# Retention and soft MoE on one core: half of the queries stay unscaled, y of three more pairs is turned by VectorE, two more key blocks are turned on chip

## The chip, the cores and the metric

The kernel runs on one core of a Trainium2 chip. The metric is the device time of one execution in microseconds; the kernel before has 152.23 us as the median of three runs (152.21 to 153.1). Below, PE is TensorE, DVE is VectorE, ACT is ScalarE, POOL is GpSimd and SP is SyncE, whose queue issues every DMA of this kernel.

## The reference

A retention layer (a linear recurrence with one decay per head) is followed by a soft mixture of experts, all in float32. Batch is 4, heads 8, sequence 768, head size 64; 32 slots, 8 experts, hidden width 1024.

```
for t in range(S):                     # per batch b and head h
    state = gamma * state + outer(k[t], v[t])
    y[t] = q[t] @ state / sqrt(64)
x = y as (4 * 768, 512)
logits = x @ phi                        # 3072 x 32
d = softmax over tokens;  slot_input = d.T @ x
slot_out[e] = relu(slot_input[e] @ w1[e]) @ w2[e]
out = softmax over slots (logits) @ slot_out
```

## The kernel before, in words

The sequence is cut into 6 chunks of 128 tokens. A step is one chunk of one batch, so there are 24 steps; two steps make a pair P, and the main loop runs over 12 pairs. Order is written by hand: every engine executes its instructions in the order of the Python code, so what stands ahead of a line on its engine is ahead of it on the chip.

In a pair, `carry_mm` multiplies the state by the queries, `attend_mm` adds the masked scores times the values, both into the PSUM banks Y0 and Y1, and `attend_copy` brings them to SBUF as `yT` (features by tokens): ACT the groups 0 and 1 (L305), DVE the groups 2 and 3 (L306). Then come `state_mm` and `state_add` (the state, bank S), and `turn_k` for the keys of the next pair. The host gives keys as features by tokens. The state needs them as tokens by features, too: for steps in `TURNED` TensorE turns them (L232) and ACT copies the result (L233), for the others the host sends them a second time and they are loaded beside the rest (`WITHK`, 512 more columns, 256 KB, in the pair's load).

The dispatch (`dispatch_u`, L424) needs y as tokens by features. There are two ways. `natural_mm` turns it on TensorE (L330, eight turns a pair) and ACT copies it (L337). `block_turn` lets DVE turn 32 by 32 blocks in place (L341), and `block_moves` puts the blocks in their places with 16 copies of 32 x 256 (L351), by ACT and POOL in turn. Pairs in `MOVED` (0, 2, 4, 6, 8) go the second way.

Decay: `decay_q` multiplies the queries of a step by the table `qtab` on POOL (L238), `decay_v` the values by powers of gamma (L243), `next_chunk` brings `qtab` to the next chunk (L246). The logits of four steps are made at odd pairs (`logits_mm`, L368), the dispatch of the four steps before them just ahead.

Loads all stand in SP's queue, in the order in which the code issues them: pair P + 3 at step P (three buffers, so it waits until pair P has been used, L227 and L221) and expert weights (`load_two`, 2 MB each, L174), as `PACE` says. After the loop, `hidden` (L667) and the second expert layer (L753) run on TensorE, the combine (L729) follows, ACT and DVE copy it out (L737), and SP stores it in eleven DMAs (L740).

Of the kernel before, what the change touches and what calls it, by code (L numbers as in the profile page):

```python
# [17 lines left out]
C = 128  # L18
# [10 lines left out]
HC = C // 2  # L29
# [14 lines left out]
NIN = 3  # L44
NRING = 9
PACE = (0, 1, 0, 1, 1, 1, 1, 1, 1, 0, 1, 0)
TURNED = (0, 1, 2, 3, 4, 6, 8, 10, 11, 12, 13, 14, 16, 18, 19)
SIW = 48
MOVED = (0, 2, 4, 6, 8)
WITHK = [[i for i in (2 * P, 2 * P + 1) if i not in TURNED and i < NSTEP - B] for P in range(NPP)]  # L50
ROWS = [[P for P in range(1, NPP - B // 2) if len(WITHK[P]) == n] for n in range(3)]
KINDS = [n for n in range(3) if ROWS[n]]
# [14 lines left out]
def constants():  # L67
    g = 1.0 - 2.0 ** (-5.0 - np.arange(H, dtype=np.float64))
    p = np.arange(128)
    k = np.zeros((128, K_PHI), np.float64)  # L70
    t = (np.arange(NC)[None, :, None] * C + p[:, None, None]).astype(np.float64)
    k[:, K_VSC:K_VSC + 48] = (g[None, None, :] ** -t).reshape(128, 48)
    gq = g[2 * np.arange(NPAIR)[None, :] + p[:, None] // HC]
    gy = g[head_of(p[:, None] // HC, np.arange(NPAIR)[None, :])]
    k[:, K_YT:K_YT + 64] = (gy[:, :, None] ** (8 * np.arange(16)) / np.sqrt(D)).reshape(128, 64)
    k[:, K_YT + 64:K_YT + 96] = (gy[:, :, None] ** np.arange(8)).reshape(128, 32)
    k[:, K_QT:K_QT + 64] = (gq[:, :, None] ** (C + 8 * np.arange(16)) / np.sqrt(D)).reshape(128, 64)
    k[:, K_QT + 64:K_QT + 96] = (gq[:, :, None] ** np.arange(8)).reshape(128, 32)
    k[:, K_GC:K_GC + NPAIR] = gq ** C
    k[:, K_J:K_J + GRP] = (p[:, None] // NSLOT) == np.arange(GRP)[None, :]  # L80
    return k.astype(np.float32)

# [2 lines left out]
def retention_soft_moe_kernel(  # L85
# [143 lines left out]
    def turn_k(i, name):  # L229
        kp = bank(name)  # L230
        for g in range(NPAIR):
            nc.tensor.transpose(kp[:, g * 128:(g + 1) * 128], st[i]["kT"][:, g, :], ident)  # L232
        nc.scalar.copy(st[i]["kn"], kp.rearrange("p (h d) -> p h d", d=D))  # L233

    def decay_q(i):
        q = st[i]["qT"]
        if i >= B:
            nc.gpsimd.tensor_tensor(q, q, qtab, ALU.mult)  # L238

    def decay_v(i, vsc=vsc, hs=((0, H),)):  # L240
        for a, b in hs:
            v = st[i]["v"][:, a:b]
            nc.gpsimd.tensor_tensor(v, v, vsc[:, i // B, a:b].unsqueeze(2).broadcast_to([128, b - a, D]), ALU.mult)  # L243

    def next_chunk():
        nc.gpsimd.tensor_tensor(qtab, qtab, gc.unsqueeze(2).broadcast_to([128, NPAIR, C]), ALU.mult)  # L246

    def score_mm(i):
        s = st[i]
# [40 lines left out]
    def attend_copy(P):  # L290
        y = pr[P]["yT"] = slot().rearrange("p (i g t) -> p i g t", i=2, t=C)
        for k in range(2):
            st[2 * P + k]["yT"] = y[:, k]
        if P < B // 2:
            for b in range(2):
                gb = slice(2 * b, 2 * b + 2)
                nc.vector.tensor_tensor(y[:, :, gb, :], pr[P]["Y"][b],
                                        ytab[:, gb, :].unsqueeze(1).broadcast_to([128, 2, 2, C]), ALU.mult)
            return
        if P == NPP - 1:  # L300
            for k in range(2):
                nc.scalar.copy(y[:, k, 0:2, :], pr[P]["y"][k][0])
                nc.vector.tensor_copy(y[:, k, 2:4, :], pr[P]["y"][k][1])
            return
        nc.scalar.copy(y[:, :, 0:2, :], pr[P]["Y"][0])  # L305
        nc.vector.tensor_copy(y[:, :, 2:4, :], pr[P]["Y"][1])  # L306

    def state_mm(P):
        S_ = pr[P]["S"] = bank("S").rearrange("p (i g e) -> p i g e", i=2, e=D)
# [7 lines left out]
    def state_add(P):  # L317
        for k in range(2):
            d = sst[(2 * P + k) % B]
            if P < B // 2:  # L320
                nc.scalar.copy(d, pr[P]["S"][:, k])
            else:
                nc.vector.tensor_tensor(d, d, pr[P]["S"][:, k], ALU.add)

    def natural_mm(P, ks=(0, 1), names=("A2", "A3")):
        X = pr[P].setdefault("X", {})
        for k in ks:
            X[k] = bank(names[k])
            for g in range(NPAIR):
                nc.tensor.transpose(X[k][:, g * 128:(g + 1) * 128], pr[P]["yT"][:, k, g, :], ident)  # L330
# [8 lines left out]
    def block_turn(P):  # L339
        x = pr[P]["xb"] = slot()  # L340
        nc.vector.transpose(x, pr[P]["yT"].rearrange("p i g t -> p (i g t)"))  # L341

    def block_moves(P, part):
        if part == 0:
            xn = pr[P]["xn"] = slot()
            for k in range(2):
                st[2 * P + k]["xn"] = xn[:, k * 512:(k + 1) * 512]
        x = pr[P]["xb"].rearrange("p (m b d) -> p m b d", b=4, d=32)
        xn = pr[P]["xn"].rearrange("p (m a d) -> p m a d", a=4, d=32)
        for n, (a, b) in enumerate((a, b) for a in (2 * part, 2 * part + 1) for b in range(4)):  # L350
            (nc.scalar.copy if n % 2 else nc.gpsimd.tensor_copy)(xn[32 * b:32 * b + 32, :, a], x[32 * a:32 * a + 32, :, b])  # L351

    gs = {}

# [146 lines left out]
    for P in range(NPP):  # L501
        last = P == NPP - 1
        g = P // 2
        if P == 0:
            load_one()
        if PACE[P] and P != NPP - 1 - NIN:
            load_two()
        if P == NPP - 2:
            take_w1(w1k[-1], load_half(slot()))
        if last:  # L510
            load_behind(P - 1)
        if P + NIN < NPP:
            load_pair(P + NIN)
            if P == NPP - 1 - NIN:
                load_two()
        else:
            weight_pool[0] = inp
        if not last:
            for i in (2 * P + 2, 2 * P + 3):
                decay_q(i)  # L520
            if P % 2 == 0 and 0 < P < NPP - 2:
                next_chunk()
            for i in (2 * P + 2, 2 * P + 3):
                decay_v(i)
            if P == 1:
                for a in range(4):
                    qd = slice(32 * a, 32 * a + 32)
                    nc.gpsimd.tensor_copy(rep[qd].rearrange("p (j s) -> p j s", s=NSLOT),
                                          ident[qd, 32 * a:32 * a + 32].unsqueeze(1).broadcast_to([32, GRP, NSLOT]))
        if P == 0:  # L530
            score_mm(2)
            attend_copy(0)
            score_mask(2)
            state_mm(0)
            state_add(0)
            score_mm(3)
            score_mask(3)
            turn_k(2, "sm")
            turn_k(3, "A0")
            decay_table(qtab, K_QT)  # L540
            block_turn(0)
            continue
        carry_mm(P)
        if last:
            take_w1(w1k[-1], load_half(sall))
        attend_mm(P)
        if last:
            load_behind(P)
            break
        attend_copy(P)  # L550
        if P < NPP - B // 2:
            state_mm(P)
            state_add(P)
        for k in range(2):
            if 2 * P + 2 + k in TURNED:
                turn_k(2 * P + 2 + k, ("A2", "Y0")[k] if P in MOVED else f"A{k}")
        if P == NPP - 2:
            block_moves(P - 2, 1)
            score_mm(2 * P + 2)
            score_mask(2 * P + 2)  # L560
            turn_mm(g - 1, "A2")
            turn_copy(g - 1)
            natural_mm(P, names=("S", "sm"))
            natural_copy(P)
            logits_bank(NGRP - 1)
            score_mm(2 * P + 3)
            score_mask(2 * P + 3)
            continue
        if P in MOVED:
            if P - 2 in MOVED:  # L570
                block_moves(P - 2, 1)
        else:
# [260 lines left out]
```

## Time and profile before

| what | value |
|---|---|
| median of the runs | 152.23 us |
| profiled execution, its own time | 152.43 us |
| its span, first to last instruction | 150.6 us |
| TensorE busy | 140.2 us, 93% of the span |
| VectorE, ScalarE, GpSimd busy | 57%, 38%, 49% |
| moved by DMA | 60.58 MB, of which 6.29 MB written |
| share of 16 DMA engines' time of the data queue | 95.8% |

Shares of busy time are averages over the whole span. Where an engine waits, the views of its waits and of the chain name what ended last. A DMA share of 1.00 means that all 16 DMA engines were moving packets throughout the stretch. A DMA counts as landed when its last part has arrived.

### The profile page before, as it was taken

How to read it: one execution, taken by the hardware profiler on the slowest of the kernel's cores; microseconds unless marked ns; L12 is line 12 of the kernel's file. 1: busy time of each engine (PE TensorE's matmuls, PEld its weight loads, DVE VectorE, ACT ScalarE, POOL GpSimd, SP SyncE). 2: the span in 40 equal slices, each digit the busy share in tenths (PEclk: the TensorE clock that was granted, in tenths of full speed). 3: DMA queues.
4: the chain of work that ended last, by engine and by line, in shares of the span. 5: the costliest groups of instructions: out<-in, count | busy, mean ns of one | idle time of the engine just before them, and what ended most of it. 6: DMA issues, size and time to landing. Idle time of an engine off the chain costs nothing.

```text
span 150.6 us, 5505 instructions
## 1 busy us (share of the span) xinstructions
PE 140.2 (93%) x2398; PEld 103.8 (69%) x2398; DVE 85.4 (57%) x192; ACT 57.0 (38%) x138; POOL 74.2 (49%) x107
## 2 busy tenths in 40 slices
PE   7999999989999999999998997999999999999830
PEld 2678989877999789978998786965232465556510
DVE  0397737792949487867869596557510101563350
ACT  3123462629172824555272708342420000352240
POOL 1182499969999989497395799700200000000000
PEclk9999999999999999999999999999999999999996
DMA  4999999999999999999999999999999999799696
GB/s 127 418 444 405 431 441 417 418 423 434 407 424 421 430 422 426 435 410 421 426 426 418 439 426 422 400 425 417 402 444 422 418 431 431 305 393 403 256 373 255
DMA packets 6936, 60.58 MB, mean 402 GB/s; under 512 B 768, under 2 KB 768, under 8 KB 3712
## 3 DMA queue, kind: packets, MB, share of 16 engines
q1 hardware_dynamic: 6912, 60.23, 95.8%
q8 instruction: 19, 0.31, 0.8%
q14 instruction: 5, 0.04, 0.1%
HBM read 53.93 MB, written 6.29 MB: 400 GB/s over the span
## 4 chain that ended last, share of the span: by engine, by line
PE 60%; DMA 26%; POOL 6%; DVE 2%; issue 2%; SPq 1%; DVEq 0%; POOLq 0%
DMA b<-in_xw_dram 12%; DMA b<-in_x_dram 10%; PE A L753 10%; PE A L253 8%; PE Y L286 8%; PE Y L667 5%; PE A L667 5%; PE S L314 4%; DMA r<-in_head_dram 3%; PE Y L277 3%; PE A L232 2%; POOL b L243 2%; PE A L330 2%; PE sm L368 2%; POOL b L238 2%
## 5 line engine op out<-in xcount | busy, mean ns | idle before, releaser
L261 DVE TENSOR_TENSOR r<-A,mi 128x512 f32<-128x512 f32 (+1 forms) x50 | 30.2, 663 | 20.3 <-PE A L253 20.3
L238 POOL TENSOR_TENSOR b<-b,qtab 128x512 f32<-128x512 f32 x20 | 25.3, 1287 | 14.0 <-DMA b<-in_x_dram 11.4
L253 PE MATMUL A<-b 64*128 64x128 f32 x384 | 25.7, 281 | 1.0 <-POOL b L238 0.8
L253 PEld LDWEIGHTS A<-b 64*128 64x128 f32 x384 | 22.8, 188 | 4.5 <-issue 1.6
L243 POOL TENSOR_TENSOR b<-b,kt 128x512 f32<-128x512 f32 x23 | 23.8, 1052 | 0.8 <-DMA b<-in_x_dram 0.8
L286 PE MATMUL Y<-r,b 128*64 128x128 f32 x352 | 22.4, 277 | 0.3 <-POOL b L243 0.3
L286 PEld LDWEIGHTS Y<-r,b 128*64 128x64 f32 x352 | 19.1, 137 | 2.7 <-issue 1.2
L351 POOL COPY r<-r 32x256 f32<-32x256 f32 x40 | 15.7, 392 | 1.6
L351 ACT COPY r<-r 32x256 f32<-32x256 f32 x40 | 16.1, 403 | 0.6
L753 PE MATMUL A<-b,r 128*32 128x128 f32 (+1 forms) x352 | 14.8, 304 | 0.1
L753 PEld LDWEIGHTS A<-b,r 128*32 128x32 f32 x352 | 9.7, 109 | 6.5 <-issue 4.2
L737 ACT COPY b<-A 128x384 f32<-128x384 f32 x10 | 4.5, 483 | 17.5 <-PE A L729 15.8
L277 PE MATMUL Y<-b,sst 64*64 64x128 f32 x304 | 10.6, 276 | 0.0
L314 PE MATMUL S<-b 128*64 128x64 f32 x304 | 10.5, 222 | 0.0
L314 PEld LDWEIGHTS S<-b 128*64 128x64 f32 x304 | 10.2, 138 | 0.0
L277 PEld LDWEIGHTS Y<-b,sst 64*64 64x64 f32 x304 | 8.2, 132 | 1.2
L470 POOL TENSOR_TENSOR cn<-cn,cz 128x128 f32<-128x128 f32 x6 | 2.4, 399 | 11.6 <-DVE cz L469 11.0
L462 ACT ACTIVATE cn<-cn 128x128 f32<-128x128 f32 x6 | 1.9, 310 | 16.4 <-DVE cn L461 16.4
L233 ACT COPY b<-A 128x512 f32<-128x512 f32 x10 | 5.8, 588 | 5.4 <-PE A L232 2.7
L306 DVE COPY r<-Y 128x512 f32<-128x512 f32 x9 | 6.2, 686 | 1.8 <-PE Y L286 1.7
L368 PEld LDWEIGHTS sm<-r,kt 128*32 128x32 f32 x192 | 5.3, 110 | 2.7 <-issue 2.7
L330 PE MATMUL A<-mi,r 128*128 128x128 f32 x48 | 6.6, 277 | 0.5 <-ACT r L305 0.4
(160 smaller groups left out, 207.9 us busy)
## 6 DMA issues: line engine op xcount, KB each, us to landing
b<-in_wtwo_dram SPq DMA_DIRECT2D x12, 2048.0 KB, 16.8
b<-in_x_dram SPq DMA_DIRECT2D x5, 1792.0 KB, 13.5
b<-in_x_dram SPq DMA_DIRECT2D x3, 1536.0 KB, 12.7
b<-in_xw_dram SPq DMA_DIRECT2D x2, 2048.0 KB, 15.6
out_dram<-b SPq DMA_DIRECT2D x5, 768.0 KB, 5.9
b<-in_wl_dram SPq DMA_DIRECT2D x2, 1536.0 KB, 11.3
r<-in_whalf_dram SPq DMA_DIRECT2D x5, 512.0 KB, 12.4
out_dram<-b SPq DMA_DIRECT2D x6, 384.0 KB, 2.9
```

The source lines that it names most:

```text
L238: nc.gpsimd.tensor_tensor(q, q, qtab, ALU.mult)
L243: nc.gpsimd.tensor_tensor(v, v, vsc[:, i // B, a:b].unsqueeze(2).broadcast_to([128, b - a, D]), ALU.mult)
L253: nc.tensor.matmul(s["sc"][r][:, g, :], s["kT"][half(r), g, :], s["qT"][half(r), g, :], start=True, stop=True, skip_group_check=True)
L261: nc.vector.tensor_tensor(s["A"][:, r, g:g + n], s["sc"][r][:, g:g + n], mask.unsqueeze(1).broadcast_to([128, n, C]), ALU.mult)
L277: nc.tensor.matmul(p["y"][k][b][half(half_of(r, g)), gl, :], sst[(2 * P + k) % B][half(r), g, :], s["qT"][half(r), g, :], start=(gl == 0 a ...
L286: nc.tensor.matmul(pr[P]["y"][k][g // 2][half(half_of(r, g)), g % 2, :], s["v"][:, 2 * g + r, :], s["A"][:, r, g, :], start=(P < B // 2 an ...
L314: nc.tensor.matmul(S_[half(r), k, g, :], s["kn"][:, 2 * g + r, :], s["v"][:, 2 * g + r, :], start=True, stop=True, skip_group_check=True)
L330: nc.tensor.transpose(X[k][:, g * 128:(g + 1) * 128], pr[P]["yT"][:, k, g, :], ident)
L351: (nc.scalar.copy if n % 2 else nc.gpsimd.tensor_copy)(xn[32 * b:32 * b + 32, :, a], x[32 * a:32 * a + 32, :, b])
L368: nc.tensor.matmul(q["ltp"][32 * j:32 * j + 32, :], phis[:, p, :], st[GRP * g + j]["yT"][:, p, :], start=(p == 0), stop=(p == NPAIR - 1), ...
L667: nc.tensor.matmul(hp[hf][32 * j:32 * j + 32, :], si0[:, a:a + NSLOT], w1t[hf, g, k][j], start=(g == 0 and k == 0), stop=(g == 1 and k == ...
L753: nc.tensor.matmul(op[32 * j:32 * j + 32, :w], hT[fc // 4][:, fc % 4, 4 * g + j, :], w2t[4 * g + j, cb, fc], start=(n == 0), stop=(n == le ...
```

## The change

Keys of steps 15 and 17 join `TURNED`, so that the host no longer sends them a second time: the loads of pairs 7 and 8 shrink by 256 KB each, and TensorE and ACT turn two more blocks of keys. Pairs 3, 5 and 7 join `MOVED`: their y no longer goes through `natural_mm` and `natural_copy`. The block turn of a pair stands now in the step behind its own, after `state_add`, and all 16 moves of that pair follow in that same step (pairs 0 and 8 excepted, which are split over two steps). `MIX` gives five of eight moves to ACT and three to POOL; the first half of pair 8 goes to ACT alone, the second to POOL alone.

`decay_q` scales the groups 0 and 1 alone. Groups 2 and 3 are scaled later, when DVE brings y out of PSUM: its copy becomes a multiplication by the same table (whose constants for these groups follow the halves of y). So `next_chunk` comes in two halves, that of groups 2 and 3 ahead of the queries of the next pair. In step 1 the weights are issued behind the load of pair 4, not ahead of it.

```diff
-TURNED = (0, 1, 2, 3, 4, 6, 8, 10, 11, 12, 13, 14, 16, 18, 19)
+TURNED = (0, 1, 2, 3, 4, 6, 8, 10, 11, 12, 13, 14, 15, 16, 17, 18, 19)
-MOVED = (0, 2, 4, 6, 8)
+MOVED = (0, 2, 3, 4, 5, 6, 7, 8)
+MIX = "sgssgssg"
+MOVES = {1: [(0, 0, MIX)], 2: [(0, 1, MIX)], 9: [(8, 0, "s")], 10: [(8, 1, "g")]}
+MOVES.update({P: [(P - 1, 0, MIX), (P - 1, 1, MIX)] for P in range(3, 9)})
...
     def decay_q(i):
         if i >= B:
-            nc.gpsimd.tensor_tensor(q, q, qtab, ALU.mult)
+            nc.gpsimd.tensor_tensor(q[:, 0:2], q[:, 0:2], qtab[:, 0:2], ALU.mult)
...
-    def next_chunk():
-        nc.gpsimd.tensor_tensor(qtab, qtab, gc.unsqueeze(2).broadcast_to([128, NPAIR, C]), ALU.mult)
+    def next_chunk(a):
+        t = qtab[:, a:a + 2]
+        nc.gpsimd.tensor_tensor(t, t, gc[:, a:a + 2].unsqueeze(2).broadcast_to([128, 2, C]), ALU.mult)
...
         nc.scalar.copy(y[:, :, 0:2, :], pr[P]["Y"][0])
-        nc.vector.tensor_copy(y[:, :, 2:4, :], pr[P]["Y"][1])
+        nc.vector.tensor_tensor(y[:, :, 2:4, :], pr[P]["Y"][1],
+                                qtab[:, 2:4].unsqueeze(1).broadcast_to([128, 2, 2, C]), ALU.mult)
...
-        if PACE[P] and P != NPP - 1 - NIN:
+        if PACE[P] and P not in (1, NPP - 1 - NIN):
             load_two()
...
             load_pair(P + NIN)
-            if P == NPP - 1 - NIN:
+            if P in (1, NPP - 1 - NIN):
                 load_two()
...
+        if P % 2 == 0 and P >= B:
+            next_chunk(2)
         if not last:
             for i in (2 * P + 2, 2 * P + 3):
                 decay_q(i)
             if P % 2 == 0 and 0 < P < NPP - 2:
-                next_chunk()
+                next_chunk(0)
...
             state_mm(P)
             state_add(P)
+        if P - 1 in MOVED:
+            block_turn(P - 1)
         for k in range(2):
             if 2 * P + 2 + k in TURNED:
-                turn_k(2 * P + 2 + k, ("A2", "Y0")[k] if P in MOVED else f"A{k}")
+                turn_k(2 * P + 2 + k, ("A2", "Y0")[k] if P % 2 == 0 else f"A{k}")
...
-        if P in MOVED:
-            if P - 2 in MOVED:
-                block_moves(P - 2, 1)
-        else:
+        if P not in MOVED:
             natural_mm(P)
             natural_copy(P)
-            block_moves(P - 1, 0)
+        for m in MOVES[P]:
+            block_moves(*m)
...
-        if P in MOVED:
-            block_turn(P)
```

The next rows are SP's queue before, from pair 2 (`b_97`) on: `in_x0_dram` and `in_x1_dram` are pairs, 128 x 3584 with one block of keys sent twice and 128 x 3072 without; pair 4 is `b_238`, and `in_wtwo_dram` are expert weights.

```order
L227 DMA b_97<-in_x1_dram 128x3584
L169 DMA b_167<-in_wone_dram 128x2048
L227 DMA b_169<-in_x1_dram 128x3584
L174 DMA b_236<-in_wtwo_dram 128x4096
L227 DMA b_238<-in_x1_dram 128x3584
L227 DMA b_367<-in_x0_dram 128x3072
```

The same place now, with pair 4 in `b_234`:

```order
L229 DMA b_97<-in_x1_dram 128x3584
L171 DMA b_167<-in_wone_dram 128x2048
L229 DMA b_169<-in_x1_dram 128x3584
L229 DMA b_234<-in_x1_dram 128x3584
L176 DMA b_236<-in_wtwo_dram 128x4096
L229 DMA b_367<-in_x0_dram 128x3072
```

Pair 4 has moved ahead of the first 2 MB of weights.

The next rows are DVE's before, from the copy of y of pair 4 to that of pair 5 and what follows (`A0` to `A3` are score banks, `r` are ring slots, L341 is the block turn).

```order
L306 COPY r_684<-Y1_651 128x2x256
L323 TENSOR_TENSOR sst_84<-sst_84,S_687 128x256 x2
L261 TENSOR_TENSOR r_740<-A0_730,mi_78 128x512
L261 TENSOR_TENSOR r_740<-A1_731,mi_78 128x512
L261 TENSOR_TENSOR r_753<-A2_743,mi_78 128x512
L261 TENSOR_TENSOR r_753<-A3_744,mi_78 128x512
L341 STREAM_TRANSPOSE r_756<-r_684 128x1024
L459 TENSOR_REDUCE cm_758<-lq_634 128x4
L461 TENSOR_TENSOR cn_760<-lq_634,cm_758 128x128
L306 COPY r_805<-Y1_772 128x2x256
L323 TENSOR_TENSOR sst_84<-sst_84,S_808 128x256 x2
L454 SCALAR_TENSOR_TENSOR acc_79<-acc_79,al_638,S_861 128x512
```

The same place now:

```order
L309 TENSOR_TENSOR r_680<-Y1_647,qtab_76 128x2x256
L327 TENSOR_TENSOR sst_84<-sst_84,S_683 128x256 x2
L345 STREAM_TRANSPOSE r_702<-r_521 128x1024
L264 TENSOR_TENSOR r_747<-A0_737,mi_78 128x512
L264 TENSOR_TENSOR r_747<-A1_738,mi_78 128x512
L264 TENSOR_TENSOR r_760<-A2_750,mi_78 128x512
L264 TENSOR_TENSOR r_760<-A3_751,mi_78 128x512
L463 TENSOR_REDUCE cm_763<-lq_629 128x4
L465 TENSOR_TENSOR cn_765<-lq_629,cm_763 128x128
L309 TENSOR_TENSOR r_810<-Y1_777,qtab_76 128x2x256
L327 TENSOR_TENSOR sst_84<-sst_84,S_813 128x256 x2
L345 STREAM_TRANSPOSE r_832<-r_680 128x1024
```

A block turn now stands in every one of these steps, ahead of the masks and not behind them, and it turns the y of the pair before.

The next rows are POOL's before, in steps 9 and 10: queries and values of pair 10 (`b_1048`), four moves, the end of a combine (`cn`), then pair 11 (`b_1207`).

```order
L238 TENSOR_TENSOR b_1048<-b_1048,qtab_76 128x512 x2
L243 TENSOR_TENSOR b_1048<-b_1048,kt_75 128x512 x2
L351 COPY r_1402<-r_1322 32x8x32 x4
L470 TENSOR_TENSOR cn_1326<-cn_1326,cz_1434 128x128
L238 TENSOR_TENSOR b_1207<-b_1207,qtab_76 128x512 x2
L243 TENSOR_TENSOR b_1207<-b_1207,kt_75 128x512 x2
L351 COPY r_1402<-r_1322 32x8x32 x4
```

The same place now (pair 10 is `b_1066`, pair 11 `b_1228`):

```order
L240 TENSOR_TENSOR b_1066<-b_1066,qtab_76 128x256 x2
L245 TENSOR_TENSOR b_1066<-b_1066,kt_75 128x512 x2
L474 TENSOR_TENSOR cn_1357<-cn_1357,cz_1467 128x128
L249 TENSOR_TENSOR qtab_76<-qtab_76,kt_75 128x256
L240 TENSOR_TENSOR b_1228<-b_1228,qtab_76 128x256 x2
L245 TENSOR_TENSOR b_1228<-b_1228,kt_75 128x512 x2
L355 COPY r_1435<-r_1420 32x8x32 x8
```

The moves have gone from ahead of pair 11's queries to behind its values, the queries are half as wide, and half a `next_chunk` has come in.

## Rows read from the trace of the kernel before

**Rows 1.** Page: busy time of TensorE, and two DMA queues (packets, MB, share).

```profile
PE 140.2 (93%) x2398; PEld 103.8 (69%) x2398; DVE 85.4 (57%) x192; ACT 57.0 (38%) x138; POOL 74.2 (49%) x107
...
q1 hardware_dynamic: 6912, 60.23, 95.8%
q8 instruction: 19, 0.31, 0.8%
```

**Rows 2.** Busy time by stretch: length, five engines, granted clock, DMA share, GB/s.

```profile
24.00:64.00 40.00, 39.29 (x777) 34.88 (x774) 28.53 (x62) 20.03 (x50) 35.11 (x48) 1.00 1.01 425
...
104.00:129.00 25.00, 24.89 (x312) 10.53 (x314) 5.74 (x22) 3.24 (x6) 0.80 (x2) 1.00 1.02 425
129.00:131.50 2.50, 2.50 (x52) 1.25 (x48) 1.27 (x3) 1.07 (x3) 0.00 (x0) 1.00 0.56 233
142.00:143.20 1.20, 0.79 (x10) 0.48 (x14) 1.14 (x3) 0.82 (x2) 0.00 (x0) 1.00 0.16 60
143.20:149.40 6.20, 1.10 (x16) 0.38 (x8) 1.95 (x4) 1.63 (x4) 0.00 (x0) 0.90 0.97 381
```

**Rows 3.** SP's timeline: last weights, sixth store, eleventh store.

```profile
112.38 0.33 SPq L174 DMA_DIRECT2D b<-in_wtwo_dram  x1
...
142.54 0.33 SPq L740 DMA_DIRECT2D out_dram<-b  x1
...
145.94 0.88 SPq L740 DMA_DIRECT2D out_dram<-b  x1
```

**Rows 4.** DMA view of the same three issues, in that order: us to landing.

```profile
b<-in_wtwo_dram SPq DMA_DIRECT2D x1, 2048.0 KB, 22.2
...
out_dram<-b SPq DMA_DIRECT2D x1, 384.0 KB, 2.3
...
out_dram<-b SPq DMA_DIRECT2D x1, 384.0 KB, 3.9
```

**Rows 5.** The chain that ended last: start us, us, what.

```profile
17.75 15.41 DMA b<-in_x_dram
...
33.92 0.87 PE A L330 x8
...
49.49 1.02 PE A L232 x8
...
65.79 17.93 DMA b<-in_xw_dram
```

**Rows 6.** TensorE's timeline, steps 3 and 10 and last L753: idle before and releaser.

```profile
33.29 0.63 PE L232 MATMUL A<-mi,b 128*128 128x128 f32 x4 [0.71 <-DMA b<-in_x_dram]
...
91.79 1.16 PE L253 MATMUL A<-b 64*128 64x128 f32 x16 [0.84 <-POOL b L238]
...
137.95 3.09 PE L753 MATMUL A<-b,r 128*32 128x128 f32 x88
```

**Rows 7.** GpSimd's timeline, steps 9 and 10.

```profile
83.88 2.52 POOL L238 TENSOR_TENSOR b<-b,qtab 128x512 f32<-128x512 f32 x2 [2.43 <-DMA b<-in_xw_dram]
86.36 2.04 POOL L243 TENSOR_TENSOR b<-b,kt 128x512 f32<-128x512 f32 x2
88.34 1.69 POOL L351 COPY r<-r 32x256 f32<-32x256 f32 x4
```

**Rows 8.** Groups by line and shape: busy us, mean ns, idle before.

```profile
L243 POOL TENSOR_TENSOR r<-r 128x256 f32<-128x256 f32 x1 | 0.6, 611 | 0.0
...
L297 DVE TENSOR_TENSOR r<-Y,acc 128x512 f32<-128x512 f32 x4 | 2.5, 674 | 0.2 <-PE Y L286 0.2
...
L306 DVE COPY r<-Y 128x512 f32<-128x512 f32 x9 | 6.2, 686 | 1.8 <-PE Y L286 1.7
...
L341 DVE STREAM_TRANSPOSE r<-r 128x1024 f32<-128x1024 f32 x5 | 6.2, 1236 | 0.0
...
L351 ACT COPY r<-r 32x256 f32<-32x256 f32 x40 | 16.1, 403 | 0.6
```

**Rows 9.** Busy time by stretch: steps 4 and 5 (columns as in Rows 2).

```profile
41.40:58.00 16.60, 16.60 (x326) 14.74 (x323) 11.86 (x27) 8.52 (x22) 15.38 (x20) 1.00 1.01 424
```

More of the change, by code (lines that the diff above doesn't have):

```diff
@@ L72, in constants @@
     k[:, K_VSC:K_VSC + 48] = (g[None, None, :] ** -t).reshape(128, 48)
-    gq = g[2 * np.arange(NPAIR)[None, :] + p[:, None] // HC]
     gy = g[head_of(p[:, None] // HC, np.arange(NPAIR)[None, :])]
@@ L76, in constants @@
     k[:, K_YT + 64:K_YT + 96] = (gy[:, :, None] ** np.arange(8)).reshape(128, 32)
-    k[:, K_QT:K_QT + 64] = (gq[:, :, None] ** (C + 8 * np.arange(16)) / np.sqrt(D)).reshape(128, 64)
-    k[:, K_QT + 64:K_QT + 96] = (gq[:, :, None] ** np.arange(8)).reshape(128, 32)
-    k[:, K_GC:K_GC + NPAIR] = gq ** C
+    k[:, K_QT:K_QT + 64] = (gy[:, :, None] ** (C + 8 * np.arange(16)) / np.sqrt(D)).reshape(128, 64)
+    k[:, K_QT + 64:K_QT + 96] = (gy[:, :, None] ** np.arange(8)).reshape(128, 32)
+    k[:, K_GC:K_GC + NPAIR] = gy ** C
     k[:, K_J:K_J + GRP] = (p[:, None] // NSLOT) == np.arange(GRP)[None, :]
@@ L302, in attend_copy @@
                 nc.scalar.copy(y[:, k, 0:2, :], pr[P]["y"][k][0])
-                nc.vector.tensor_copy(y[:, k, 2:4, :], pr[P]["y"][k][1])
+                nc.vector.tensor_tensor(y[:, k, 2:4, :], pr[P]["y"][k][1], qtab[:, 2:4], ALU.mult)
             return
         nc.scalar.copy(y[:, :, 0:2, :], pr[P]["Y"][0])
-        nc.vector.tensor_copy(y[:, :, 2:4, :], pr[P]["Y"][1])
+        nc.vector.tensor_tensor(y[:, :, 2:4, :], pr[P]["Y"][1],
+                                qtab[:, 2:4].unsqueeze(1).broadcast_to([128, 2, 2, C]), ALU.mult)
     def state_mm(P):
@@ L341, in block_turn, with block_moves @@
         nc.vector.transpose(x, pr[P]["yT"].rearrange("p i g t -> p (i g t)"))
-    def block_moves(P, part):
+    def block_moves(P, part, on="sg"):
         if part == 0:
@@ L350, in block_moves @@
         for n, (a, b) in enumerate((a, b) for a in (2 * part, 2 * part + 1) for b in range(4)):
-            (nc.scalar.copy if n % 2 else nc.gpsimd.tensor_copy)(xn[32 * b:32 * b + 32, :, a], x[32 * a:32 * a + 32, :, b])
+            {"s": nc.scalar.copy, "g": nc.gpsimd.tensor_copy}[on[n % len(on)]](xn[32 * b:32 * b + 32, :, a], x[32 * a:32 * a + 32, :, b])
     gs = {}
@@ L540, in retention_soft_moe_kernel @@
             decay_table(qtab, K_QT)
-            block_turn(0)
             continue
@@ L568, in retention_soft_moe_kernel @@
             continue
-        if P in MOVED:
-            if P - 2 in MOVED:
-                block_moves(P - 2, 1)
-        else:
+        if P not in MOVED:
             natural_mm(P)
             natural_copy(P)
-            block_moves(P - 1, 0)
+        for m in MOVES[P]:
+            block_moves(*m)
         if P % 2 == 0 and P > 0:
@@ L602, in retention_soft_moe_kernel @@
     siT = qtab.rearrange("p g t -> p (g t)")[:, 0:2 * (NK * SIW + 16)]
-    nc.gpsimd.memset(siT, 0.0)
     siT = siT.rearrange("p (g x) -> p g x", g=2)
@@ L608, in retention_soft_moe_kernel @@
     attend_copy(NPP - 1)
+    nc.gpsimd.memset(si0[:, 0:2 * (NK * SIW + 16)], 0.0)
     natural_mm(NPP - 1, (0,))
```

## Prediction, made before the run

> **What bounds the kernel now.** The page alone says TensorE: busy 93% of the span [rows 1]. It also says that the data queue takes 95.8% of the time of all 16 DMA engines, so I read the busy time by stretch next, where the reader should look at the column of the DMA share: 1.01 and 1.02 in stretches that cover 24 to 64 and 104 to 129 us, at 425 GB/s, with TensorE nearly as full [rows 2]. Both run without a break for most of the kernel; which of them sets the end has to be read at the end.
>
> There, SP's timeline and the DMA view belong together: issue plus time to landing is the landing. The last 2 MB of weights are issued at 112.38 and land 22.2 us later, at 134.6 [rows 3, 4]. Yet between 129 and 131.5 the 16 engines are only 0.56 busy [rows 2]: some had done their part of these weights and had no more work, while others were still at theirs. A DMA counts as landed with its last part, so the last engine is the clock. A likely cause of the difference is that a second queue brings instructions over the same engines: 19 packets, 0.8% of 16 engines' time, so 0.008 x 16 x 150.6 / 19 = 1.0 us each [rows 1], and they need not fall evenly. The same again at the stores: from 142.0 to 143.2 the share is 0.16 [rows 2], so two or three engines are still at the fifth store while the others wait for TensorE's last results. From then to 149.4 all are full (0.97). The sixth store, issued at 142.54, lands after 2.3 us; the eleventh, issued at 145.94, needs 3.9 us and lands at 149.8 [rows 3, 4]. It is 1.6 us late because it stands behind the other stores. The span ends 0.8 us later, at 150.6.
>
> So the last DMA engines have work without a break from the first loads to 149.8, and **their sum of bytes sets the end**. TensorE is close behind. Had the last engines no lag, the others, filled from 143.2 on by six stores, would end at 149.4: about 0.4 us earlier, with TensorE as it is.
>
> **The change, part by part.**
>
> *Bytes.* Two key blocks of 256 KB are no longer loaded: 2 x 262,144 B = 0.524 MB, at 425 GB/s [rows 2] 1.23 us for every one of the 16 engines alike. Nothing else of the traffic changes: weights, stores and sizes are the same. SP's order changes in one place. Pair 4 cannot be issued before pair 1 is used up, at 17.75 [rows 5], and now holds the first 2.1 MB of `load_two` back until then. The queue then still holds the weights `wone` and pair 3, which by the share of 1.01 keep the engines busy, so I cost this at nothing; if that cover were gone it would cost at most what these weights take themselves, 2.1 / 0.425 = 4.9 us.
>
> *TensorE.* Out go three `natural_mm` of eight turns, 0.87 us each [rows 5]: 2.6 us. In come two `turn_k`; eight such turns take 1.02 us [rows 5], so 1.0 us. At 33.29 TensorE waits 0.71 us for pair 4 [rows 6], which lands at 17.75 + 15.41 = 33.16 [rows 5]. Ahead of 2.1 MB of weights it lands 2.1 / 0.425 = 4.9 us earlier, so the wait goes. Next late there is the dispatch, which without `natural_mm` comes to bank S before `state_add` has emptied it: I allow 0.35 us. Up to step 9 TensorE gains 2.6 - 1.0 + 0.7 - 0.35 = 2.0 us.
>
> *GpSimd in steps 9 and 10.* Pair 10 lands at 65.79 + 17.93 = 83.72 [rows 5]; GpSimd then does two queries (2.52), two values (2.04), four moves (1.69), a small combine and the first queries of pair 11 [rows 7], and TensorE waits for those at 91.79 [rows 6]. Now pair 10 lands 1.23 earlier, at 82.5. A half-width product took 0.61 us [rows 8], so: two queries 1.3, values 2.04, half a `next_chunk` 0.6, the combine as before; ready before 87. Pair 11 lands 2.1 MB behind pair 10, at 82.5 + 4.9 = 87.4, and is then the last. With its half query, 0.65, the scores can start at 88.1 instead of 91.8. TensorE itself is there at about 88. From here on it is 3.5 us ahead; what follows in the tail is unchanged.
>
> *The engines that take over.* DVE gets three block turns of 1.24 us [rows 8], and every turn now stands behind `state_add` and ahead of the masks. The masks wait for the scores, which TensorE starts after key turns (and at odd steps after dispatch and logits): 3 us or more after `attend_mm` ends, and copy, state and turn take 0.7 + 1.05 + 1.24 = 3.0. Cost zero; if the cover is gone, up to 1.24 us a step. The product that replaces the copy of y reads PSUM and one SBUF table like L297, 674 ns against the copy's 686 [rows 8]: nothing. ACT pays most: in the 16.6 us of steps 4 and 5 it was busy for 8.52 us [rows 9]; 12 more moves of 403 ns [rows 8], two natural copies of 0.6 us less and some turned keys make some 12.4 of then 15.5 us. Behind the moves on ACT stand the copy of the dispatch weights (L409) and the next copy of y. By my count the moves end 7.2 us after `attend_mm` of an even step and the dispatch of the next odd step needs L409 at 9.1: 1.6 us of cover after that copy. Cost zero.
>
> *The sum.* TensorE gains 3.5 us, the last DMA engines 1.23 us. The last weights land at 133.4. They are the second half of the last block of L753, of 128 products, of which the last 88 started at 137.95 and took 3.09 us [rows 6]: the 65th stood at 138.8 and would stand at 135.3, so there is no wait. The stores, issued 3.5 us earlier, queue behind the last engines: the eleventh, issued at 142.4, lands at 148.6, after 6 us. The end is that of the engines: span 150.6 - 1.2 = 149.4. The profiled execution took 152.43, so it would take 151.2; against the median, 152.23 - 1.23 = **151.0 us**, 0.8% less. This needs of TensorE only 1.2 - 0.4 = 0.8 us of its 3.5.
>
> **A rule against it.** The rows say that TensorE's 93% and the queue's 95.8% are within three points, and that the tail is decided by single engines. The Trainium skill, page "Trace Analysis", section "Identifying the Most-Contended Engine", says to judge DMA by the bytes moved per time and not by occupancy, since 16 engines make occupancy misleading, and to work on the engine that is highest. By that page's 435 GB/s or so for 16 engines, the 400 GB/s of this span are an estimated 92%, TensorE would be the bound, and the sum would be TensorE's gain. The landing of the eleventh store does not agree with it, so I keep the engines' sum.
>
> **The rivals.**
>
> *The end follows TensorE.* If the lag of the last engines is not a fixed load but is made up when the stores come earlier, or their late packets are instructions that fall elsewhere in the new program, the end moves with TensorE: 152.2 - 3.5 = 148.7. For it: 0.56 and 0.16 [rows 2] show most engines with time to spare. Against: each engine's part of every DMA is the same, so a late engine cannot give work away. One instruction packet and its disturbance fewer on the last engine would already give about 149.5 to 150.
>
> *Half of it is lost.* The covers above hold in part, TensorE gains less than 0.8 us, or an instruction packet more falls on the last engine: 151.4 to 152.3. For it: several covers are 0.1 to 0.5 us wide. Against: GpSimd's relief alone, 3 us and more, stands ahead of the tail.
>
> *ScalarE becomes the bound.* If the moves end later than I have them, for instance because each waits for GpSimd's share or for the block turn, L409 comes late and TensorE waits for it at steps 3, 5, 7 and 9. It starts to cost at 1.6 us of lateness a step and makes the kernel slower than before from about 2.5 us on (four times 0.9 eats the 3.5). With 3.2 us: four times 1.6 is 6.4, less 3.5 and less the 0.4 of the engines' lag, 152.2 + 2.5 = 154.7. For it: ACT at 80%, in order, with waits at both ends. Against: 403 ns a move is steady over 40 of them [rows 8].
>
> *Not as said.* That SP's swap opens a gap in the loads would show as a DMA share under 1 at 18 to 28 us; it is in the second rival's chance.
>
> **How the numbers follow.** Forecast 0.67 (150.6 to 151.5, from 1.1 to 1.4 us of bytes and half a percent of spread), end follows TensorE 0.13 (148.7 to 150.3), half lost 0.14, ScalarE 0.06. A measurement of this kernel tells about 1% from no change, which is 150.7 and 153.75 us. Faster by more than 1%: 0.13 and a tenth of the forecast, 0.20. Slower by more: 0.05 of ScalarE's. The rest, 0.75, within 1%. The range leaves out the lower half of the second case and the upper of the last: 150.0 to 152.3.
>
> **What would show it.** Pairs 7 and 8 land some 3.7 us behind the weights ahead of them, and pair 10 at 82.5. The wait at 33.29 is gone, the first scores of pair 11 start near 88. The stores are issued about 3.5 us earlier but the eleventh needs about 6 us to land, at 148.6: if it needs under 4, the end followed TensorE. Waits of L424 for ACT at odd steps would show the ScalarE case; a DMA share under 1 before 125 us would break the sum of bytes.

## The result, and the profile after

| | before | after |
|---|---|---|
| median of 7 runs | 152.27 us | 150.77 us (150.48 to 151.97) |
| ratio, 95% interval | | 0.9895 [0.9862, 0.9929] |
| profiled execution, its span | 152.43, 150.6 us | 150.77, 149.1 us |

The change saves 1.0%, 1.5 us; forecast were 151.0 us and 0.8%, in a range of 150.0 to 152.3. Two numbers of the working came out as forecast: the last weights land at 111.08 + 22.1 = 133.2 (said: 133.4), and the scores of pair 11 start at 88.27 (said: 88.1). Behind these two, the way to the end was another one.

The page of the kernel after, busy time and two DMA queues, answers to [rows 1]: 0.53 MB less on the data queue, 2.2 us less on TensorE, 13 us more on ACT.

```profile
PE 138.0 (93%) x2382; PEld 102.3 (69%) x2382; DVE 89.2 (60%) x195; ACT 70.1 (47%) x172; POOL 68.1 (46%) x121
...
q1 hardware_dynamic: 6912, 59.70, 96.2%
q8 instruction: 19, 0.31, 0.8%
```

Busy time by stretch of the kernel after, columns as in [rows 2]. The first, second and third stretch show the queue still full (share 0.99 to 1.01). The other three are those of [rows 2] at the end, moved up by 1.5 us: the lag of single engines is still there (0.62 and 0.27).

```profile
24.00:64.00 40.00, 39.58 (x803) 35.31 (x799) 31.77 (x65) 29.02 (x74) 33.01 (x57) 1.00 1.01 423
41.40:58.00 16.60, 16.60 (x322) 14.85 (x320) 14.38 (x31) 12.61 (x32) 14.00 (x24) 1.00 1.01 420
104.00:129.00 25.00, 24.89 (x334) 10.81 (x326) 5.66 (x21) 3.59 (x7) 0.80 (x2) 1.00 0.99 416
127.50:130.00 2.50, 2.50 (x46) 1.21 (x49) 1.08 (x3) 0.87 (x3) 0.00 (x0) 1.00 0.62 262
140.50:141.70 1.20, 0.79 (x10) 0.53 (x13) 0.86 (x3) 0.54 (x2) 0.00 (x0) 1.00 0.27 101
141.70:147.70 6.00, 0.82 (x12) 0.20 (x4) 1.95 (x4) 1.63 (x4) 0.00 (x0) 0.93 0.98 387
```

The second line answers to [rows 9]: ACT is busy for 12.61 us where 12.4 were expected, and TensorE for all 16.60.

SP's timeline of the kernel after: last weights, sixth and eleventh store, as in [rows 3].

```profile
111.08 0.33 SPq L176 DMA_DIRECT2D b<-in_wtwo_dram  x1
...
140.76 0.33 SPq L744 DMA_DIRECT2D out_dram<-b  x1
...
144.36 0.89 SPq L744 DMA_DIRECT2D out_dram<-b  x1
```

The DMA view of the same three issues, as in [rows 4]; the last column is us to landing.

```profile
b<-in_wtwo_dram SPq DMA_DIRECT2D x1, 2048.0 KB, 22.1
...
out_dram<-b SPq DMA_DIRECT2D x1, 384.0 KB, 2.9
...
out_dram<-b SPq DMA_DIRECT2D x1, 384.0 KB, 3.9
```

The eleventh store is issued 1.58 us earlier than before, not 3.5, and needs 3.9 us, as before, not 6. Where TensorE's lead went, its own timeline shows (columns as in [rows 6]):

```profile
33.42 1.06 PE L428 MATMUL S<-r,pl 128*32 128x512 f32 x8 [0.42 <-DVE sst L327]
...
88.27 1.16 PE L256 MATMUL A<-b 64*128 64x128 f32 x16
...
92.62 1.09 PE L289 MATMUL Y<-r,b 128*64 128x128 f32 x16
95.12 0.43 PE L289 MATMUL A<-r,b 128*64 128x128 f32 x2 [1.41 <-DVE r L264]
...
103.09 1.49 PE L671 MATMUL A<-b,qtab 128*32 128x512 f32 x12
```

At 88.27 TensorE is 3.52 us ahead of before (91.79, [rows 6]). At the first product of `hidden`, L671, it is only 1.30 us ahead (103.09 against 104.39). The same two places in TensorE's timeline of before, the last `attend_mm` (L286) and `hidden` (L667):

```profile
96.14 1.09 PE L286 MATMUL Y<-r,b 128*64 128x128 f32 x16
...
104.39 1.92 PE L667 MATMUL A<-b,qtab 128*32 128x512 f32 x16
```

So 2.2 us are lost, in the last `attend_mm`, which waits for the mask of step 23 (L264). VectorE's timeline says what the mask waited for:

```profile
94.38 1.29 DVE L264 TENSOR_TENSOR r<-A,mi 128x512 f32<-128x512 f32 x2 [2.89 <-POOL r L355]
```

And GpSimd's timeline, steps 9 and 10, answers to [rows 7]:

```profile
82.36 1.43 POOL L240 TENSOR_TENSOR b<-b,qtab 128x256 f32<-128x256 f32 x2 [3.03 <-DMA b<-in_xw_dram]
83.75 2.04 POOL L245 TENSOR_TENSOR b<-b,kt 128x512 f32<-128x512 f32 x2
...
87.40 1.41 POOL L240 TENSOR_TENSOR b<-b,qtab 128x256 f32<-128x256 f32 x2 [0.68 <-DMA b<-in_xw_dram]
88.78 2.04 POOL L245 TENSOR_TENSOR b<-b,kt 128x512 f32<-128x512 f32 x2
90.88 3.46 POOL L355 COPY r<-r 32x256 f32<-32x256 f32 x8
```

The mask writes into a new slot of the ring `r`. That slot still holds the block-turned y of pair 8, which GpSimd reads in the last eight moves, from 90.88 to 94.34. The mask starts at 94.38.

In the kernel before, too, half of pair 8's moves stood in step 10, four on ACT and four on GpSimd. There the same mask (L261) did not wait for them: it runs beside GpSimd's four, so it had another slot. The two lines are from VectorE's and from GpSimd's timeline of before:

```profile
95.20 1.29 DVE L261 TENSOR_TENSOR r<-A,mi 128x512 f32<-128x512 f32 x2 [0.20 <-PE A L253]
...
95.02 1.70 POOL L351 COPY r<-r 32x256 f32<-32x256 f32 x4
```

So the eight moves did not only go to GpSimd. With the block turn one step later, the order in which slots are taken and given back is another one, too, and the slot that the moves read is now the one that the mask takes next. The chain that ended last runs through this place. In before it left GpSimd with the queries of pair 11, at 91.75; now it stays there until 94.35 and goes on over the mask:

```profile
72.99 14.28 DMA b<-in_xw_dram
87.40 1.41 POOL b L240 x2
...
93.94 0.41 POOL r L355
94.38 1.30 DVE r L264 x2
95.72 0.54 PE A L289 x5
```

Last, the groups by line and shape, against [rows 8]: the moves on ACT keep their 402 ns, a half query takes 735 ns, the block turn 1238 and the product in the copy's place 692.

```profile
L355 ACT COPY r<-r 32x256 f32<-32x256 f32 x78 | 31.4, 402 | 3.1 <-DVE r L345 2.2
...
L240 POOL TENSOR_TENSOR b<-b,qtab 128x256 f32<-128x256 f32 x20 | 14.3, 735 | 13.0 <-DMA b<-in_x_dram 9.2 <-DMA b<-in_xw_dram 3.7
...
L345 DVE STREAM_TRANSPOSE r<-r 128x1024 f32<-128x1024 f32 x8 | 9.9, 1238 | 0.0
...
L309 DVE TENSOR_TENSOR r<-Y,qtab 128x512 f32<-128x512 f32 x9 | 6.2, 692 | 4.6 <-PE Y L289 4.6
```

### The profile page after: what moved, and what is told of

The parts are those of the page before. It is cut to its first block, busy times and chain, and to the rows that moved or that the text cites. A ratio compares the mean times of both kernels' runs of the same rounds, so it can differ in the third digit from the quotient of the medians.

```text
span 149.1 us, 5532 instructions
## 1 busy us (share of the span) xinstructions
PE 138.0 (93%) x2382; PEld 102.3 (69%) x2382; DVE 89.2 (60%) x195; ACT 70.1 (47%) x172; POOL 68.1 (46%) x121
## 4 chain that ended last, share of the span: by engine, by line
PE 61%; DMA 23%; POOL 6%; DVE 4%; issue 1%; SPq 1%; DVEq 0%; POOLq 0%
DMA b<-in_x_dram 10%; DMA b<-in_xw_dram 10%; PE A L757 10%; PE Y L289 8%; PE A L256 8%; PE Y L671 5%; PE A L671 5%; PE S L318 5%; PE Y L280 3%; DMA r<-in_head_dram 3%; PE sm L372 3%; PE A L234 2%; POOL r L355 2%; POOL b L245 2%; PE sm L733 2%; DVE b L741 2%
## 5 line engine op out<-in xcount | busy, mean ns | idle before, releaser
L264 DVE TENSOR_TENSOR r<-A,mi 128x512 f32<-128x512 f32 (+1 forms) x50 | 30.2, 662 | 16.3 <-PE A L256 13.4
L355 ACT COPY r<-r 32x256 f32<-32x256 f32 x78 | 31.4, 402 | 3.1 <-DVE r L345 2.2
L355 POOL COPY r<-r 32x256 f32<-32x256 f32 x50 | 19.8, 395 | 6.9 <-PE S L428 2.8
L240 POOL TENSOR_TENSOR b<-b,qtab 128x256 f32<-128x256 f32 x20 | 14.3, 735 | 13.0 <-DMA b<-in_x_dram 9.2
L741 ACT COPY b<-A 128x384 f32<-128x384 f32 x10 | 4.5, 483 | 17.0 <-PE A L733 15.3
L345 DVE STREAM_TRANSPOSE r<-r 128x1024 f32<-128x1024 f32 x8 | 9.9, 1238 | 0.0
L309 DVE TENSOR_TENSOR r<-Y,qtab 128x512 f32<-128x512 f32 x9 | 6.2, 692 | 4.6 <-PE Y L289 4.6
L235 ACT COPY b<-A 128x512 f32<-128x512 f32 x11 | 6.3, 588 | 5.7 <-PE A L234 2.3
L327 DVE TENSOR_TENSOR sst<-sst,S 128x256 f32<-128x256 f32 x16 | 6.0, 418 | 1.9 <-PE S L318 1.9
L671 PE MATMUL A<-b,qtab 128*32 128x512 f32 x64 | 7.1, 594 | 0.0
```

The costliest lines, as they stand in the source:

```text
L240: nc.gpsimd.tensor_tensor(q[:, 0:2], q[:, 0:2], qtab[:, 0:2], ALU.mult)
L264: nc.vector.tensor_tensor(s["A"][:, r, g:g + n], s["sc"][r][:, g:g + n], mask.unsqueeze(1).broadcast_to([128, n, C]), ALU.mult)
L355: {"s": nc.scalar.copy, "g": nc.gpsimd.tensor_copy}[on[n % len(on)]](xn[32 * b:32 * b + 32, :, a], x[32 * a:32 * a + 32, :, b])
L671: nc.tensor.matmul(hp[hf][32 * j:32 * j + 32, :], si0[:, a:a + NSLOT], w1t[hf, g, k][j], start=(g == 0 and k == 0), stop=(g == 1 and k == ...
```

## The experiments

So the time came out as forecast, but the eleventh store, by the prediction's own sign (under 4 us), says that TensorE set the end. Two theories stood against each other. **A**: the last DMA engines set a floor, a time that the bytes need whatever TensorE does, and the kernel after has just reached it. **B**: the end follows TensorE, and had the 2.2 us not been lost, the kernel would be near 148.8. This table has all runs. Its three middle columns are from one profiled execution each; the ratio is to the kernel before on the same chip. In e9 and e10 the first product of `hidden` is that behind the last idle product.

| kernel | first product of `hidden` | 11th store issued | us to landing | ratio, 95% interval |
|---|---|---|---|---|
| before | 104.39 | 145.94 | 3.9 | 1 |
| after | 103.09 | 144.36 | 3.9 | 0.9895 [0.9862, 0.9929] |
| e1_moves9 | 101.90 | 142.98 | 5.5 | 0.9901 [0.9873, 0.9928] |
| e2_keys_back | 102.08 | 144.17 | 4.9 | 0.9952 [0.9932, 0.9972] |
| e3_idle_load | 103.12 | 144.50 | 5.0 | 0.9983 [0.9962, 1.0004] |
| e4_bytes_alone | 104.14 | 145.44 | 3.9 | 0.9969 [0.9946, 0.9992] |
| e5_full_queries | 101.88 | 142.95 | 4.9 | 0.9858 [0.9811, 0.9905] |
| e8_key9_turned | 101.85 | 142.93 | 4.8 | 0.9856 [0.9801, 0.9912] |
| e7_all_turned | 104.00 | 145.35 | 3.9 | 0.9858 [0.9799, 0.9918] |
| e9_warm3 | 102.17 | 143.21 | 4.6 | 0.9879 [0.984, 0.9919] |
| e10_warm8 | 103.89 | 145.11 | 3.9 | 0.9952 [0.9926, 0.9978] |

The executions don't all start alike: pair 3's load is issued at 12.65 in after, at 13.73 in e1 and 14.54 in e7. Points in time of different rows are to be compared to about 1 us only (to 2 us with e7), and where TensorE is late in one execution, the time to landing is shorter for it; the ratios come from other executions, too, and suffer less. Nor is the issue of the eleventh store TensorE's alone: where stores pile up, SP takes longer over each issue (0.87 us for the ninth and the tenth in e2).

**e1_moves9: give TensorE the lost time back.** Pair 8's last moves go to ACT, one step earlier, so that the slot comes free.

```diff
-MOVES = {1: [(0, 0, MIX)], 2: [(0, 1, MIX)], 9: [(8, 0, "s")], 10: [(8, 1, "g")]}
+MOVES = {1: [(0, 0, MIX)], 2: [(0, 1, MIX)], 9: [(8, 0, "s"), (8, 1, "s")], 10: []}
```

> All 16 moves of pair 8 go to ACT in step 9, none to GpSimd in step 10, so that the mask of step 23 finds its ring slot free. Both theories: VectorE's wait for the moves (2.9 us) goes, and the first L671 starts near 101 instead of 103.1. Theory A (the DMA engines that are last set the end): the last weights still land at 133.2 and the time falls by 0.4 us at most, to 150.3 to 150.8. Theory B (the end follows TensorE's stores): the time falls by as much as TensorE gains, to about 148.8.

TensorE's timeline of e1 in the same place has no wait left. From the last `attend_mm` to `hidden` it takes 8.24 us (93.66 to 101.90); after took 10.47 (92.62 to 103.09), before 8.25.

```profile
93.66 1.09 PE L289 MATMUL Y<-r,b 128*64 128x128 f32 x16
94.58 0.61 PE L289 MATMUL A<-r,b 128*64 128x128 f32 x8
...
101.90 4.50 PE L671 MATMUL A<-b,qtab 128*32 128x512 f32 x40
```

The slot was the cause of the loss. But the 150.93 us are no gain on after (150.77). The DMA view of e1 shows why, with its eleventh store, issued at 142.98 in this execution:

```profile
out_dram<-b SPq DMA_DIRECT2D x1, 384.0 KB, 5.5
```

Before and after needed 3.9. What the other 1.6 us are, the last stretch ahead of the landing shows; the next rows are busy time by stretch, columns as in [rows 2], of before, after, e1, e2 and e10, in that order.

```profile
147.90:149.40 1.50, 0.00 (x0) 0.00 (x0) 0.00 (x0) 0.00 (x0) 0.00 (x0) 0.59 0.94 371
...
146.20:147.70 1.50, 0.00 (x0) 0.00 (x0) 0.00 (x0) 0.00 (x0) 0.00 (x0) 0.73 0.97 385
...
146.50:148.10 1.60, 0.00 (x0) 0.00 (x0) 0.00 (x0) 0.00 (x0) 0.00 (x0) 0.50 0.11 42
...
147.50:148.70 1.20, 0.00 (x0) 0.00 (x0) 0.00 (x0) 0.00 (x0) 0.00 (x0) 0.50 0.13 51
...
147.00:148.40 1.40, 0.00 (x0) 0.00 (x0) 0.00 (x0) 0.00 (x0) 0.00 (x0) 0.50 0.99 395
```

In before and after all 16 DMA engines work to the end (0.94 and 0.97): there is no engine that lags, and the end is TensorE's last results and the 16 engines' time for the last stores. In e1 the share is 0.11 for the last 1.6 us. That is about two engines of 16, alone at work while every other engine of the core has nothing left to do. These two are theory A's floor, and they are against B.

**e2_keys_back: e1 with the keys of steps 15 and 17 loaded again.** TensorE has still its lead; the bytes are those of before.

```diff
-TURNED = (0, 1, 2, 3, 4, 6, 8, 10, 11, 12, 13, 14, 15, 16, 17, 18, 19)
+TURNED = (0, 1, 2, 3, 4, 6, 8, 10, 11, 12, 13, 14, 16, 18, 19)
```

> As the run before, and the keys of steps 15 and 17 are loaded again instead of turned (0.524 MB back, TensorE spared 1.0 us). Theory A: the last weights land at 134.5 as in the kernel before, and the time is 151.7 to 152.1 although TensorE is over 2 us ahead of the kernel before. Theory B: pair 11 lands 1.2 us later, so that TensorE is some 2.4 us ahead of the kernel before: about 149.9.

Measured 151.72 us, 0.5% (0.8 us) over e1, with intervals that don't meet; A had said 151.7 to 152.1. TensorE reaches `hidden` 2.3 us before the kernel before does, and the last copy ahead of the eleventh store (L741, in before L737) ends 2.8 us before (142.84 against 145.62), but only 0.5% comes of it. The last weights land at 134.34, as before (134.57), and again about two engines work alone at the end (0.13). At the same bytes, this 0.5%, some 0.7 us, is then what TensorE was late by in the kernel before.

**e3_idle_load: after, and 0.524 MB more that nobody reads,** behind the last weights.

```diff
     assert not weights
+    extra = large(big)
+    nc.sync.dma_start(extra[:, 0:1024], whalf[0])
```

> The changed kernel with one more load of 0.524 MB behind the last weights, ahead of the stores; nobody reads it, and TensorE's work is the same. Theory A: every engine has 1.23 us more to move ahead of the stores; 0.8 to 1.2 us longer than the changed kernel, 151.6 to 152.0. Theory B: the engines have spare time there (share 0.62 at 127.5 to 130), so no more than 0.2 us longer, 150.8 to 151.0.

TensorE is where it was in after (103.12), the time is 152.3: 0.9% more, some 1.3 us. SP's timeline and the DMA view of e3 have the idle load, which lands at 113.55 + 21.1 = 134.6, 1.2 us behind the last weights (133.4):

```profile
113.55 0.33 SPq L708 DMA_DIRECT2D b<-in_whalf_dram  x1
```

```profile
b<-in_whalf_dram SPq DMA_DIRECT2D x1, 512.0 KB, 21.1
```

The stores pay for it, with 5.0 us for the eleventh. Bytes alone cost time in this kernel: for A. 1.3 us is a little over the 0.8 to 1.2 that A had said, and over the 1.23 of half a MB by 425 GB/s; by the intervals that is no difference.

**e4_bytes_alone: before with the two keys turned,** and nothing else (the edit of e2 the other way round).

> The kernel before with nothing but the keys of steps 15 and 17 turned instead of loaded. Theory A: the last weights land 1.2 us earlier than in the kernel before, the stores follow as far as TensorE lets them (pair 10 lands 1.2 us earlier, GpSimd's chain behind it as well): 151.0, the whole gain of the change. Theory B: TensorE gains 1.2 at step 10 by pair 10's landing, less whatever of the 1.0 us of turns isn't hidden: 151.0 to 151.6.

This missed: 152.04 us, 0.3%. The last weights land at 133.13, 1.4 us earlier than before, but `hidden` starts at 104.14, 0.25 earlier, and the eleventh store, 0.50 earlier, needs 3.9 us. In this kernel TensorE is the later one, as it was in before: its scores wait for pair 11's values at 93.77, for 0.36 us. The bytes are worth something only as far as TensorE comes along.

**e9_warm3, e10_warm8: take TensorE's lead away again.** e1 with more idle products (L482) ahead of `hidden`, loads untouched; three calls in e9, as shown, and eight in e10.

```diff
-    warm(1, "A0")
+    warm(3, "A0")
```

> This is e1_moves9 with two more calls of the idle product (L482) just ahead of the hidden layer, nothing else: TensorE reaches the first product of L671 later, by 0.52 us for each call (the profile of e1 shows 0.51 from the start of the one call to the first L671), so by 1.0 us, at 102.9 instead of 101.9. Loads and bytes are the same. Theory A (the last DMA engines set the end; in e1 the eleventh store needed 5.5 us to land where it needs 3.9 when TensorE is the later one, so TensorE has about 1.6 us to spare): the last weights land at 133.2 as before, the eleventh store is issued 1.0 later and needs 1.0 less, and the time is e1's, 150.7 to 151.1. Theory B (the end follows TensorE): 1.0 us more than e1, 151.9 to 152.1.

> e1_moves9 with seven more calls of the idle product ahead of the hidden layer: TensorE is 7 x 0.52 = 3.6 us later at the first L671, 105.5. Theory A: 1.6 us of it is TensorE's spare time, the other 2.0 us is paid: 152.7 to 153.1, with a store that needs 3.9 us to land. Theory B (the end follows TensorE): all 3.6 us is paid, 154.3 to 154.7. If the time is e1's still, TensorE has far more to spare than either theory says.

The idle products were cheaper than said. From the products of L650 to the first store it takes 27.83 us in e1, 28.59 in e9 and 30.76 in e10: 0.8 and 2.9 us later. The 0.8 cost nothing (150.58 us, against 150.93). The 2.9 cost 0.5%, 0.8 us (151.75), with an interval that begins about where e1's ends and clear of e9's. TensorE's timeline of e10, and the eleventh store in its DMA view:

```profile
100.41 3.42 PE L482 MATMUL A<-const-float32-0.0 128*1 128x256 f32 x15
...
103.89 1.49 PE L671 MATMUL A<-b,qtab 128*32 128x512 f32 x12
```

```profile
out_dram<-b SPq DMA_DIRECT2D x1, 384.0 KB, 3.9
```

e10 lies 1.0 us under A's forecast of 152.7 to 153.1; 0.7 of that is the idle products, which took 2.9 us and not 3.6. Of the 2.9 A leaves 2.9 - 1.6 = 1.3 us to be paid and B all; paid were 0.8. This is A, with some 2 us of room in e1 if TensorE pays in full behind it. That it does is what e10's last stretch suggests, where all 16 engines work to the end (0.99), but one step of this size can't show it alone.

**e5_full_queries: e1 with all queries scaled as before.** `decay_q`, `next_chunk`, the table's constants and the copy of y are those of the kernel before.

```diff
-            nc.gpsimd.tensor_tensor(q[:, 0:2], q[:, 0:2], qtab[:, 0:2], ALU.mult)
+            nc.gpsimd.tensor_tensor(q, q, qtab, ALU.mult)
...
-        nc.vector.tensor_tensor(y[:, :, 2:4, :], pr[P]["Y"][1], ...)
+        nc.vector.tensor_copy(y[:, :, 2:4, :], pr[P]["Y"][1])
```

> As e1_moves9, but the queries of all four groups are scaled on GpSimd as in the kernel before, y is copied by VectorE and next_chunk is whole. GpSimd's two queries cost 2.5 instead of 1.4 us a step, so that in steps 9 and 10 TensorE should be 0.6 to 1.2 us later than in e1_moves9 (first L671 at 102.5 to 103.1 instead of 101.9). Theory A (the last DMA engines set the end, TensorE only where it is later): TensorE's spare 1 us or so covers this, the last weights land at 133.2, and the time is that of e1_moves9 within 0.4 us: 150.7 to 151.2. Theory B (the end follows TensorE): 151.5 to 152.1.

A's time was met: 150.75 us, no later than e1 or after. The scores of pair 11 start at 89.28, 1.0 us behind after (both loaded pair 3 at 12.65), and the room of e1 swallows it. With pair 8's moves as in e1, the half queries are not needed for the gain: GpSimd goes on to the queries of pair 11 at 87.18, where before four moves held them up (88.34, [rows 7]), since pair 8's moves are all on ACT here.

**e8_key9_turned, e7_all_turned: more keys turned instead of loaded,** on top of e1: step 9 in e8, as shown, and all twenty in e7.

```diff
-TURNED = (0, 1, 2, 3, 4, 6, 8, 10, 11, 12, 13, 14, 15, 16, 17, 18, 19)
+TURNED = (0, 1, 2, 3, 4, 6, 8, 9, 10, 11, 12, 13, 14, 15, 16, 17, 18, 19)
```

> As e1_moves9, and the keys of step 9 are turned as well: 0.262 MB less to load, 0.5 us more for TensorE. Theory A: the last weights land at 132.6 and the end comes 0.6 us earlier than in e1_moves9: 150.3. Theory B: no gain, or 0.5 us lost: 150.9 to 151.4.

> As e1_moves9, and the keys of steps 5, 7 and 9 are turned as well, so that no key is loaded twice: 0.786 MB less, 1.85 us for each DMA engine, 1.5 us more for TensorE. Theory A: the last weights land at 131.3; the engines alone would allow 1.8 us less, but TensorE, at the first L671 near 102.5, then is the later one, as the end lay 45.0 us behind the first L667 in the kernel before: time 149.9 to 150.3. Theory B: TensorE loses up to 1.5 us: 151.0 to 152.4.

e8 took 150.72 us, e7 150.84. Their intervals, 0.980 to 0.991 and 0.992, are too wide to tell them from e1 or after, or to decide on the 150.3, and 149.9 to 150.3, that A had said. In e8 the last weights land at 132.76 and in e7 at 131.39, as expected. In e7 the stores again need 3.9 us: in this execution, with fewer bytes, TensorE, which got the turns and started late, is the later one. Its profiled execution took 151.76 where its median is 150.84, so its points in time say less than its ratio.

## Why the prediction was right, and where not

**What bounds it: right in kind, the order was wrong.** The prediction had the last DMA engines at the end of the kernel before, and TensorE 0.4 us behind. e2 and e3 show that the engines' bytes are a bound: they cost time at a TensorE that is no later. But in before it was TensorE that came later, by the 0.5% (0.7 us) that e2 gains at the same bytes, and e4 shows the same: bytes without TensorE give 0.3%. The 0.4 us was read from 149.4, where the engines are full, to 149.8, where the eleventh store lands. All 16 are full up to 149.4, though (0.94), and behind that no engine starts another packet, as the same view of before says:

```profile
149.50:149.80 0.30, 0.00 (x0) 0.00 (x0) 0.00 (x0) 0.00 (x0) 0.00 (x0) 0.50 0.00 0
```

After has the same 0.3 us ahead of its landing (147.90 to 148.20, share 0.00), with no engine late. So the 0.4 us is no lag of single engines.

The end is the later of two times. One is the engines' floor, which the change brought down; the other is TensorE's, from its last results on. With the bytes of after, up to an issue of the eleventh store near 144.4 the time stays at 150.6 to 150.9 (after, e1, e5, e9); e10, issued at 145.11, is 151.75.

**The bytes: right, the price about so.** 1.23 us were forecast. The last weights land 1.37 us earlier (134.57 to 133.20); in time, e1 against e2 gives 0.8 us and e3 against after 1.3.

**TensorE: the step that failed** is "From here on it is 3.5 us ahead; what follows in the tail is unchanged". Up to 88.27 it was right to 0.2 us; the 0.35 us allowed for the dispatch was 0.42 (at 33.42; the key turns of pair 4 start at 32.34 without a wait). But the prediction only took the moves away from ahead of pair 11's queries. It gave no price to the eight behind its values, and did not ask whose slot they read. The mask of step 23 needed that slot: 2.2 us lost, which e1 gives back by moving them.

**The time: in part luck.** The 1.5 us are not 1.23 of bytes with TensorE to spare. Before and after both end with TensorE's last stores, and the eleventh is issued 1.58 us earlier: the gain is what was left of TensorE's lead. That this is also about as far as the floor allows is chance. A smaller loss would have bought nothing (e1, e5 and e9 are no faster), a larger one would have cost time (e10). The split by the runs is 0.5% for TensorE down to the old floor (e2) and 0.5% for the bytes (e1 against e2).

**The stores: the sizes failed with it.** "The eleventh, issued at 142.4, lands at 148.6, after 6 us" became 144.36, 148.24 and 3.9 us. e1 is the case that was described: 142.98, 148.48 and 5.5 us.

**The engines that take over: right.** The block turns stay off the path, the product costs 692 against 686 ns. In steps 4 and 5 ACT's moves end at 47.3 and TensorE does not wait there at all (16.60 busy of 16.60), so the rival with ScalarE did not come. The half query was put at 0.65 us and took 0.73; by e5 it didn't matter. SP's swap left no gap: the share from 18 to 28, where one would have shown, is 1.02.

**The rule against it.** The Trainium skill, page "Perfetto Trace Analysis", section "Identifying the Most-Contended Engine", judges DMA by bytes per time. From this the prediction concluded that TensorE, with 93%, was the bound, and 148.7 the time. That is not what the section says: for TensorE it does not take the busy share of products, but FLOPs and the busy share of weight loads. The weight loads are 69% here ([rows 1], PEld), under the 92% that the prediction estimated for the DMA. So the rule was no argument for 148.7. What bytes per time can't tell is which engine is last: just before the last weights land the 16 engines of after are 0.62 busy on average, at 262 GB/s, and half a MB more in that place still cost e3 0.9%.

**What stays open** is why some DMA engines lag behind others. The prediction's guess, instruction packets that fall unevenly, was not tried: no edit here moves them without moving the program too.

## What to carry to other kernels

When two engines run full to the end, price an edit by both, and expect the smaller of the two gains. Two signs told here which one was met: the time from the last store's issue to its landing, and the DMA share over the last microsecond, near 1 when the stores wait for results and far under it when single DMA engines are late. When work goes to another step or engine, look not only at who waits behind it there, but at the buffers that it reads: in a ring, the next writer of that slot may be far away and on the path. And try the parts of a change one by one behind the result: here the halved queries were worth nothing that could be measured, once pair 8's moves were out of the way.

## What was unexpected on the chip

The bare time from issue to landing of the eleventh store of 384 KB was 3.9 us in five of the eleven profiles, though the bytes themselves are 0.9 us by 425 GB/s: it stands behind five others, issued from 140.76 on in after. And a product of 128 x 256 took GpSimd 735 ns in L240 but 614 in L249: the same engine, operation and size, 0.12 us apart. L240 multiplies by a full table, L249 by one constant for each group and row, repeated over its 128 tokens. The kernel before has the same pair at 128 x 512, 1287 ns (L238) against 1040 (L246). So the time goes with the second operand here, but no run changes that alone.
